# A convolution by DFTs and two gated MLPs on one core: inputs 4 to 15 of the transform come in quarters of 128 KB, not in halves of 256 KB

## The chip, the cores and the metric

One core of one Trainium2 chip. The metric is the device time of one execution in microseconds (us). The kernel before took 1119.01 us, the median of three runs (1118.45 to 1119.3).

## The reference

```
X = rfft(x, axis=1);  F = filt_r + 1j * filt_i            # x: 2 x 3008 x 256
y = irfft(X * F, n=3008, axis=1)                          # the transform: 16 inputs of 512 KB here
h = (silu(y @ w_gate) * (y @ w_val)) @ w_out              # 256 -> 1536 -> 256
g = h @ w_in
out = (g * clip(g + 3, 0, 6) / 6) @ w_out2                # 256 -> 2048 -> 256
```

All in float32 on 6016 tokens of 256 channels.

## The kernel before, in words

The sequence of 3008 is treated as a grid of 47 x 64. A transform **step** k (0 to 15) handles one batch and 32 channels: `over_n1` (DFT over the 47 rows, 64 small matmuls, L334), `over_n2` (over the 64 columns, 16 matmuls, L356), `filter_product` (VectorE and GpSimd multiply by the filter, L369), `back` (inverse over the columns, 16 matmuls, L383, ScalarE copies into `turned`, L388). The loop starts with `over_n1(k)`, then `back(k - 2)`, then the transfers that the table `moves` holds for step k, then `over_n2(k)` and `filter_product(k)`. After step 15 the results, which went through DRAM (tiles `d2_0`, `d2_1`, shown as `d`), are read back as `g`, `y` and `turned` tiles, `to_time` (L158) finishes the inverse, and the MLPs begin on TensorE (L234, L242, later L706 and L751), which are most of the time.

Everything is written in program order; no scheduler moves instructions. The transfers nearly all stand on SyncE's queue (SP), which issues them strictly in order; each waits until what it overwrites has been read. Every DMA also signals one of eight completion semaphores (DMAHW0 to DMAHW7 in the instruction order), handed out in turn, and waits at its issue until the transfer that used the same one, eight transfers earlier, has landed. So at most eight are on their way.

What the change and the prediction touch:

- `load_x(k)` (L286 to L295) brings input k, 512 KB, into the tile `ring`, which holds four inputs; input k + 3 is asked for in step k, after `over_n1(k)`, and overwrites input k - 1. Inputs 0 and 1 come with both halves of the channels in each piece, the others by channel halves.
- `load_filter(j)` (L299, 2 x 192 KB): filter 2 is asked for in step 2, filters 3 to 7 in steps 4 to 8. `prepare_filter` (L326, VectorE) uses it one or two steps later.
- `load_dec` (L406, 3 x 256 KB): the raw first weights, pieces in steps 1, 2, 3, then 8, 9, 9, then 12, 12, 13. ScalarE starts the first decoding in step 4 (L189).
- `store` (L392, 192 KB): parts of `turned` to DRAM, eight of the first channel half of batch 0 in steps 9 to 12, eight of the second in step 13.
- `load_half` (L464): reads them back; the second half's reads wait for all stores and are needed by `form(0, 1)` (L158 on `g`) right after `back(15)`.

Of the kernel before, what the change touches and what calls it, by code (L numbers as in the profile page):

```python
# [77 lines left out]
def fft_conv_glu_mlp(ctx: ExitStack, tc: tile.TileContext, x, filt, mats, sgn, w1, w2, out):  # L78
# [189 lines left out]
    with tc.manual_schedule():  # L268
# [17 lines left out]
        def load_x(k, engines=(nc.sync, nc.sync)):  # L286
            b, j = STEPS[k]
            if k % 2 == 0:
                xin[k // 2] = ring[:, k // 2 % RING * 2048:(k // 2 % RING + 1) * 2048].rearrange("p (a n) -> p a n", a=2)
            to, src = (v.rearrange("p (o i n) -> p i o n", o=2, i=2) if k < 2 else v.rearrange("p (i n) -> p i n", i=2)  # L290
                       for v in (xin[k // 2][:, k % 2], x[b, j // 2, :, j % 2]))
            for i in range(2):
                if (k, i) == (1, 1):
                    nc.sync.dma_start(out=mat[:, CO:], in_=mats[:, CO:])
                engines[i].dma_start(out=to[:, i], in_=src[:, i])  # L295

        def load_filter(j):
            for r in range(2):
                nc.sync.dma_start(out=fl[j // 4][:, j % 4, r], in_=filt[j][:, r])  # L299

        load_x(0, (nc.scalar, nc.sync))
        load_x(1, (nc.scalar, nc.sync))
        nc.sync.dma_start(out=sg, in_=sgn)
        load_filter(0)
        load_x(2)
        warm = keep.tile([P, 32], F32, name="warm")[:, 0:1]
        nc.gpsimd.memset(warm, 0.0)
# [282 lines left out]
        for t in range(2 * plain):  # L590
            p, i = divmod(t, 2)
            k, g_ = steps[p]
# [163 lines left out]
        class Plain:  # L756
            kind, k, f, n, last = 0, 0, 0, 512, True
# [105 lines left out]
        pieces = [(g, i) for g in range(G2) for i in range(2)]  # L863
# [19 lines left out]
        for s in range(S):  # L883
# [15 lines left out]
            k, f, n, kind = u.k, u.f, u.n, u.kind  # L899
# [73 lines left out]
        for j, accs in enumerate((banks["a"][1], banks["a"][3])):  # L973
            to, at = ys[k][:, ORDER.index(2 * j + 1), :n], pos[k] + n
# [52 lines left out]
```

## Time and profile before

| | |
|---|---|
| median of three runs | 1119.01 us |
| the profiled execution | 1118.54 us |
| its span (first to last instruction) | 1116.7 us |
| outside the span | 1.84 us |
| TensorE (PE) busy | 1107.7 us, 99% of the span |
| VectorE, ScalarE, GpSimd busy | 863.3, 750.4, 598.0 us |
| granted clock of TensorE | 0.999 |

The transform fills about the first 70 us. A row of the timeline gives start, length, engine, line, operation, tiles and count, and in brackets how long the engine stood idle before it and what ended that ("issue": nothing that the profile shows). PEld are TensorE's weight loads, SPq is SyncE's queue of DMA issues.

### The profile page before, as it was taken

The numbers are of one execution on the slowest core, as the hardware profiler recorded it, in microseconds if no ns is written. First come the engines' busy times: TensorE is split into PE (matmuls) and PEld (weight loads), VectorE is DVE, ScalarE is ACT, GpSimd is POOL, SyncE is SP. The second block draws the span as 40 slices with busy tenths as digits, with TensorE's granted clock in tenths as the row PEclk, the third lists the DMA queues.
The fourth block names the chain that finished last, engine by engine and source line by source line (L and its number), as shares of the span: only waits on it lengthen the run. The fifth ranks groups of instructions, "written<-read, shape, count | busy, mean of one in ns | idle before, by whom it ended". The sixth has DMA issues, their size and how long they took to land.

```text
span 1116.7 us, 19188 instructions
## 1 busy us (share of the span) xinstructions
PE 1107.7 (99%) x7237; PEld 921.4 (83%) x7237; DVE 863.3 (77%) x1179; ACT 750.4 (67%) x1363; POOL 598.0 (54%) x773
## 2 busy tenths in 40 slices
PE   8999999999999999999999999999999999999998
PEld 6778888888888888888899888888888888888997
DVE  5999977878878888786898868677677677677765
ACT  4655447667667667766777777777776677677764
POOL 3742376795865576474587645335435444354440
PEclk9999999999999999999999999999999999999999
DMA  8977845843733553273353421422322412412300
GB/s 272 286 222 227 256 157 170 232 143 131 192 121 113 155 165 100 83 203 113 103 207 111 171 81 55 152 78 77 129 78 78 145 61 78 149 52 78 116 27 33
DMA packets 58988, 150.75 MB, mean 135 GB/s; under 512 B 5712, under 2 KB 26160, under 8 KB 57136
## 3 DMA queue, kind: packets, MB, share of 16 engines
q1 hardware_dynamic: 58208, 148.78, 41.9%
q8 instruction: 56, 0.92, 0.4%
q10 hardware_dynamic: 688, 0.75, 0.2%
q14 instruction: 36, 0.29, 0.1%
HBM read 117.27 MB, written 32.24 MB: 134 GB/s over the span
## 4 chain that ended last, share of the span: by engine, by line
PE 93%; DVE 3%; DMA 2%; issue 1%; SPq 1%; ACT 0%; DVEq 0%; ACTq 0%
PE gv L706 44%; PE a L751 36%; PE gv L234 5%; PE a L242 3%; PE gv L158 1%; PE gv L383 1%; PE a L356 1%; PE gv L334 1%; DMA d<-turned 1%; DVE h L733 1%; DVE hs L116 1%; DMA ring<-x_in 0%; SPq L392 0%; DVE xs L116 0%; DMA g<-d 0%
## 5 line engine op out<-in xcount | busy, mean ns | idle before, releaser
L706 PE MATMUL gv<-xs,wu 128*128 128x512 f32 (+1 forms) x2268 | 567.1, 386 | 0.2 <-DVE gv L119 0.2
L116 POOL TENSOR_TENSOR wu<-st,wu 128x224 fp32r<-128x224 f32 x432 | 310.3, 749 | 396.2 <-ACT wu L539 396.2
L706 PEld LDWEIGHTS gv<-xs,wu 128*128 128x128 f32 x2268 | 423.6, 188 | 81.7 <-DVE h L119 1.8
L751 PE MATMUL a<-hs,wo 128*128 128x512 f32 (+1 forms) x1872 | 476.9, 385 | 0.0
L751 PEld LDWEIGHTS a<-hs,wo 128*128 128x128 f32 x1872 | 351.3, 188 | 65.6 <-ACT hs L739 0.3
L116 DVE TENSOR_TENSOR hs<-h,hs 128x512 fp32r<-128x512 f32 (+3 forms) x228 | 235.4, 1033 | 65.3 <-ACT hs L739 61.1
L739 ACT CAST hs<-h 128x512 fp32r<-128x512 f32 (+3 forms) x216 | 172.6, 799 | 130.0 <-DVE h L735 73.8
L116 POOL TENSOR_TENSOR wo<-st,wo 128x256 fp32r<-128x256 f32 x156 | 150.6, 978 | 0.0
L735 DVE SCALAR_TENSOR_TENSOR h<-h,gv 128x512 f32<-128x512 f32 (+1 forms) x144 | 96.5, 670 | 23.0 <-ACT h L729 22.8
L539 ACT CAST wu<-st 128x384 fp32r<-128x384 f32 x216 | 110.6, 563 | 0.6 <-DMA st<-w1f 0.6
L727 ACT ACTIVATE h<-gv 128x512 f32<-128x512 f32 (+1 forms) x120 | 70.6, 588 | 56.8 <-PE gv L706 55.6
L119 DVE TENSOR_TENSOR gv<-gv,h 128x512 f32<-128x512 f32 (+1 forms) x108 | 74.0, 685 | 40.2 <-PE gv L706 34.1
L729 ACT ACTIVATE h<-gv 128x512 f32<-128x512 f32 (+1 forms) x144 | 84.1, 584 | 15.5 <-PE gv L706 15.4
L916 ACT COPY gv<-gv 128x512 f32<-128x512 f32 (+1 forms) x108 | 60.9, 564 | 42.3 <-PE gv L706 38.5
L119 DVE TENSOR_TENSOR h<-gv,h 128x512 f32<-128x512 f32 (+1 forms) x108 | 73.0, 676 | 18.5 <-PE gv L706 17.9
L735 DVE SCALAR_TENSOR_TENSOR h<-h,h 128x512 f32<-128x512 f32 (+1 forms) x48 | 32.7, 681 | 58.6 <-ACT h L729 58.6
L920 ACT COPY h<-gv 128x512 f32<-128x512 f32 (+1 forms) x108 | 62.5, 579 | 15.8 <-PE gv L706 12.6
L733 DVE TENSOR_TENSOR h<-h 128x512 f32<-128x512 f32 (+1 forms) x60 | 61.5, 1024 | 1.7 <-ACT h L727 1.2
L116 DVE TENSOR_TENSOR xs<-raw,xs 128x512 fp32r<-128x512 f32 (+1 forms) x77 | 57.9, 753 | 0.1
L539 ACT CAST wo<-st 128x256 fp32r<-128x256 f32 (+1 forms) x108 | 54.1, 501 | 0.0
L582 ACT CAST xs<-raw 128x512 fp32r<-128x512 f32 (+1 forms) x77 | 45.7, 609 | 3.1 <-DVE raw L116 3.0
L234 PE MATMUL gv<-xs,wall_a 128*128 128x512 f32 x192 | 45.9, 393 | 0.2 <-ACT xs L123 0.2
(98 smaller groups left out, 893.9 us busy)
## 6 DMA issues: line engine op xcount, KB each, us to landing
st<-w1f SPq DMA_DIRECT2D x60, 576.0 KB, 3.8
st<-w2f SPq DMA_DIRECT2D x48, 704.0 KB, 4.1
raw<-w_in SPq DMA_DIRECT2D x16, 512.0 KB, 4.6
ring<-x_in SPq DMA_DIRECT2D x30, 256.0 KB, 5.2
x<-w_in SPq DMA_DIRECT2D x9, 768.0 KB, 5.6
yd<-y SPq DMA_DIRECT2D x5, 1024.0 KB, 6.7
raw<-yd SPq DMA_DIRECT2D x5, 1024.0 KB, 6.7
y_out<-y SPq DMA_DIRECT2D x20, 256.0 KB, 2.1
```

Source lines behind the costliest of these rows:

```text
L116: (engine or nc.vector).tensor_tensor(out=out, in0=a, in1=b, op=ALU.subtract)
L119: (engine or nc.vector).tensor_tensor(out=out, in0=a, in1=b, op=ALU.add)
L234: nc.tensor.matmul(acc, w[:, r, c[k]:c[k] + P], xs[:, v, k], start=(r, v, k) == (0, 0, 0), stop=(r, k) == (1, 1), skip_group_check=len(dep ...
L539: nc.scalar.copy(out=to[:, 0, at:at + hi - lo], in_=src[:, lo:hi])
L706: nc.tensor.matmul(acc[:, :n], w[:, r, FORM[a] * P:(FORM[a] + 1) * P], xs_part(k, v, i), start=start and q == 0, stop=q == 2, skip_group_c ...
L727: nc.scalar.activation(out=self.value(t, 0), in_=src, func=AF.Silu)
L729: nc.scalar.activation(out=self.value(t, a), in_=src, func=AF.Relu, bias=3.0)
L733: nc.vector.tensor_tensor(out=self.value(t, 0), in0=self.value(t, 0), in1=src, op=ALU.mult)
L735: nc.vector.scalar_tensor_tensor(out=self.value(t, a), in0=self.value(t, a), scalar=6.0, in1=src, op0=ALU.min, op1=ALU.mult)
L739: nc.scalar.copy(out=self.hs[:, t, :, 0, :self.n], in_=self.value(t))
L751: yield lambda t=t, v=v, a=a, j=j, r=r: nc.tensor.matmul(banks["a"][2 * j + t][:, :n], self.wo[:, r, (2 * a + j) * P:(2 * a + j + 1) * P], ...
L920: nc.scalar.copy(out=u.s7, in_=b3[:, :n])
```

## The change

For inputs 4 to 15 `load_x` cuts the 1024 floats of each partition into four pieces, not two, and issues the four DMAs one behind the other on SP. Inputs 0 to 3 stay as they are, and so does what each input brings and where it is put.

```diff
             b, j = STEPS[k]
             if k % 2 == 0:
                 xin[k // 2] = ring[:, k // 2 % RING * 2048:(k // 2 % RING + 1) * 2048].rearrange("p (a n) -> p a n", a=2)
-            to, src = (v.rearrange("p (o i n) -> p i o n", o=2, i=2) if k < 2 else v.rearrange("p (i n) -> p i n", i=2)
+            pieces = 2 if k < 4 else 4
+            to, src = (v.rearrange("p (o i n) -> p i o n", o=2, i=2) if k < 2 else v.rearrange("p (i n) -> p i n", i=pieces)
                        for v in (xin[k // 2][:, k % 2], x[b, j // 2, :, j % 2]))
-            for i in range(2):
+            for i in range(pieces):
                 if (k, i) == (1, 1):
                     nc.sync.dma_start(out=mat[:, CO:], in_=mats[:, CO:])
-                engines[i].dma_start(out=to[:, i], in_=src[:, i])
+                engines[i % 2].dma_start(out=to[:, i], in_=src[:, i])
```

SP's queue from input 4 on, in steps 1 and 2, before (128x512 on `ring` is half an input, `w_in` a piece of the raw first weights, `filt_in` half of a filter; in brackets the semaphores waited for, DMAHWn being the landing of the transfer eight places earlier):

```order
L295 DMA ring<-x_in 128x512 [waits DMAHW7_49,PE_49]
L295 DMA ring<-x_in 128x512 [waits DMAHW0_49,PE_49]
L406 DMA x_121<-w_in 128x512 [waits DMAHW1_49]
L295 DMA ring<-x_in 128x512 [waits DMAHW2_49,PE_49]
L295 DMA ring<-x_in 128x512 [waits DMAHW3_49,PE_49]
L406 DMA x_121<-w_in 128x512 [waits DMAHW4_49]
L299 DMA x_121<-filt_in 128x384 [waits DMAHW5_49]
L299 DMA x_121<-filt_in 128x384 [waits DMAHW6_49]
```

The same place in the changed kernel:

```order
L296 DMA ring<-x_in 128x256 [waits DMAHW7_49,PE_49]
L296 DMA ring<-x_in 128x256 [waits DMAHW0_49,PE_49]
L296 DMA ring<-x_in 128x256 [waits DMAHW1_49]
L296 DMA ring<-x_in 128x256 [waits DMAHW2_49,PE_49]
L407 DMA x_121<-w_in 128x512 [waits DMAHW3_49]
L296 DMA ring<-x_in 128x256 [waits DMAHW4_49,PE_49]
L296 DMA ring<-x_in 128x256 [waits DMAHW5_49,PE_49]
L296 DMA ring<-x_in 128x256 [waits DMAHW6_49]
L296 DMA ring<-x_in 128x256 [waits DMAHW7_49,PE_49]
L407 DMA x_121<-w_in 128x512 [waits DMAHW0_49]
L300 DMA x_121<-filt_in 128x384 [waits DMAHW1_49]
L300 DMA x_121<-filt_in 128x384 [waits DMAHW2_49]
```

Filter 2 moves back by four places on SP, and the transfer eight places ahead of it is now a quarter of input 4, not a half of input 3.

SP's queue at the end of the inputs, step 12, before (input 15, two pieces of weights, the last store of the first channel half, `d` from `turned`, and after the last weight piece the first read back):

```order
L295 DMA ring<-x_in 128x512 [waits DMAHW6_49,PE_49]
L295 DMA ring<-x_in 128x512 [waits DMAHW7_49,PE_49]
L406 DMA x_121<-w_in 128x512 [waits DMAHW0_49,DVE_49]
L406 DMA x_121<-w_in 128x512 [waits DMAHW1_49]
L392 DMA d_0_78<-turned 128x3x128 [waits DMAHW2_49]
L406 DMA x_121<-w_in 128x512 [waits DMAHW3_49]
L464 DMA g<-d_0_78 48x6x128 [waits DMAHW5_49,DMAHW4_49,DMAHW2_49]
```

And in the changed kernel:

```order
L296 DMA ring<-x_in 128x256 [waits DMAHW4_49,PE_49]
L296 DMA ring<-x_in 128x256 [waits DMAHW5_49,PE_49]
L296 DMA ring<-x_in 128x256 [waits DMAHW6_49]
L296 DMA ring<-x_in 128x256 [waits DMAHW7_49,PE_49]
L407 DMA x_121<-w_in 128x512 [waits DMAHW0_49,DVE_49]
L407 DMA x_121<-w_in 128x512 [waits DMAHW1_49]
L393 DMA d_0_78<-turned 128x3x128 [waits DMAHW2_49]
L407 DMA x_121<-w_in 128x512 [waits DMAHW3_49]
L465 DMA g<-d_0_78 48x6x128 [waits DMAHW4_49,DMAHW2_49]
```

By then 24 more DMAs have been issued (363 rows on SP, 339 before); the four of an input stand where two stood, and everything behind them keeps its order. The instructions of the other engines stay in their order.

## Rows read from the trace of the kernel before

**Rows 1.** The page, busy time, share of the span and instructions.

```profile
PE 1107.7 (99%) x7237; PEld 921.4 (83%) x7237; DVE 863.3 (77%) x1179; ACT 750.4 (67%) x1363; POOL 598.0 (54%) x773
```

**Rows 2.** Waits of TensorE, 8 to 75 us: us in total, times, longest.

```profile
PE a L356 <- issue: 2.2, 1, 2.2
PE gv L334 <- issue: 0.8, 1, 0.8
```

**Rows 3.** Timeline of TensorE, 17.3 to 20.5 us.

```profile
17.27 0.81 PE L356 MATMUL a<-y,mat 64*64 64x384 f32 x4
20.33 0.55 PE L356 MATMUL a<-y,mat 64*64 64x384 f32 x4 [2.25 <-issue]
```

**Rows 4.** Timeline of TensorE, 43 to 46 us.

```profile
45.33 0.39 PE L334 MATMUL gv<-mat,ring 48*64 48x48 f32 x12 [0.83 <-issue]
```

**Rows 5.** The page, DMA queues: packets, MB, share of 16 engines.

```profile
q8 instruction: 56, 0.92, 0.4%
```

**Rows 6.** DMA queues, 12 to 18 us.

```profile
q1 hardware_dynamic: 986, 1.76, 91.7%
```

**Rows 7.** DMA queues, 18 to 19.1 us.

```profile
q8 instruction: 1, 0.02, 5.5%
```

**Rows 8.** DMA queues, 43 to 44.1 us.

```profile
q8 instruction: 1, 0.02, 5.6%
```

**Rows 9.** Timeline of SP's issues, 8.2 to 13.5 us.

```profile
8.34 2.82 SPq L295 DMA_DIRECT2D ring<-x_in  x4
11.21 0.43 SPq L406 DMA_DIRECT2D x<-w_in  x1
11.73 0.86 SPq L295 DMA_DIRECT2D ring<-x_in  x2
```

**Rows 10.** Windows: engines' busy time (count), clock, DMA share, GB/s.

```profile
14.00:20.50 6.50, 4.25 (x106) 3.19 (x102) 3.37 (x8) 2.97 (x8) 2.83 (x6) 1.00 1.04 361
```

**Rows 11.** DMA packets by size, 6 to 7.5 us.

```profile
DMA packets 614, 0.56 MB, mean 371 GB/s; under 512 B 175, under 2 KB 611, under 8 KB 614
```

**Rows 12.** Waits of SP's queue, 8 to 55 us.

```profile
SPq L295 <- PE gv L334: 7.1, 8, 1.4
SPq L295 <- DMA ring<-x_in: 4.1, 4, 1.8
...
SPq L392 <- DMA ring<-x_in: 1.0, 3, 0.4
```

**Rows 13.** DMA issues, 16.5 to 17 us: KB each, median us to landing.

```profile
x<-w_in SPq DMA_DIRECT2D x1, 256.0 KB, 7.4
```

**Rows 14.** Timeline of ScalarE, 23.5 to 28 us.

```profile
24.79 0.95 ACT L189 ACTIVATE x<-x 128x768 f32<-128x768 f32 x1
26.45 0.48 ACT L347 COPY y<-gv 128x384 f32<-128x384 f32 x1 [0.72 <-PE gv L334]
26.83 0.34 ACT L348 ACTIVATE y<-gv 128x192 f32<-128x192 f32 x1
```

**Rows 15.** Chain of waits, 49 to 60 us: start, us, what.

```profile
51.26 6.02 DMA d<-turned
```

**Rows 16.** DMA issues, 68 to 69.7 us.

```profile
g<-d SPq DMA_DIRECT2D x2, 144.0 KB, 3.2
turned<-d SPq DMA_DIRECT2D x2, 144.0 KB, 4.3
```

**Rows 17.** Timeline, 58 to 80 us, SP's second reads and TensorE's use.

```profile
68.30 0.82 SPq L464 DMA_DIRECT2D g<-d  x2
...
73.64 0.84 PE L158 MATMUL a<-mat,g 48*64 48x47 f32 x48
```

**Rows 18.** Timeline of TensorE, two successive steps.

```profile
27.35 1.75 PE L356 MATMUL a<-y,mat 64*64 64x384 f32 x16
...
31.00 1.75 PE L356 MATMUL a<-y,mat 64*64 64x384 f32 x16
```

**Rows 19.** DMA issues, 0 to 60 us.

```profile
ring<-x_in SPq DMA_DIRECT2D x30, 256.0 KB, 5.2
```

## The prediction

> **What bounds the kernel now.** I read the busy times first: TensorE is busy for 99% of the span, no other engine over 77% [rows 1]. So time is won or lost only where TensorE stands still. The change touches the transform, and there the waits of TensorE say what there is to win: from 8 to 75 us it stood still for 2.2 us once and 0.8 us once, both put down to "issue", that is, to nothing that the profile shows; no wait for an input is among them [rows 2]. The inputs themselves come in time, so cutting them finer can't win by bringing the first quarter sooner.
>
> The two stalls need a reason. They are 2.25 us before 20.33 [rows 3] and 0.83 us before 45.33 [rows 4]. The DMA queue of kind "instruction", q8, moved 56 packets of together 0.92 MB [rows 5]; divided by the 7237 + 7237 instructions of TensorE and its weight loads that is 64 bytes each, and about 258 instructions a packet. So I take q8 for TensorE's own program. From 12 to 18 us no packet of it moved while q1, the data, had the DMA engines for 91.7% [rows 6]; one packet moved in the 1.1 us behind [rows 7], and TensorE went on at 20.33. The same stands before the second stall: one packet between 43 and 44.1 us [rows 8], TensorE going on at 45.33. My reading is that both stalls are a wait for the next piece of program, which came late behind queued data. That is inference from the times alone; the profile names no cause.
>
> How much data is queued? SP issued seven transfers of 256 KB from 8.34 to 12.59: four and two of `ring` and one of weights [rows 9]. From 14 to 20.5 us the DMA engines were full and moved 361 GB/s [rows 10].
>
> **The change, part by part.** Removed are 24 issues of 256 KB, added 48 of 128 KB: the bytes are the same, SP has 24 issues more.
>
> Moving the bytes. Rows of 1 KB per partition are half as long. Between 6 and 7.5 us nearly all packets were under 2 KB (611 of 614) and 371 GB/s were reached [rows 11], no less than the 361 with rows mostly of 2 KB. Bounds: no cost, or, if the extra completion of each transfer costs the engines a tenth of a microsecond (my estimate; no row isolates it), 0.2 us for each input. I take 0.1, beside other work unless the transfers are the bound.
>
> SP's time. Two issues of `ring` take 0.86 us [rows 9], so 0.43 each and 24 x 0.43 = 10.3 us more. What hides it is SP's own waiting between 8 and 55 us: 7.1 us for TensorE to free an input, and 4.1 and 1.0 us for a landing eight transfers back [rows 12], 12.2 us in these three rows. Sum: 10.3 against 12.2, so SP should end about as early, but with hardly any slack; in steps with seven issues it will run late by itself. Queued behind are filter 2, the weights, the stores and the read backs.
>
> The first stall. At the time when the missing program should have been asked for, about 12 us, seven transfers had gone out: 7 x 256 = 1792 KB. With the same rhythm of issues the changed kernel has sent two halves of input 3, four quarters of input 4 and one piece of weights: 2 x 256 + 4 x 128 + 256 = 1280 KB. 512 KB less, at 361 GB/s, is 1.45 us. So the stall should fall from 2.25 to 0.8 us if the program waits behind the data already queued. Bounds: 0, if it doesn't, and 2.25.
>
> The second stall. Again up to eight transfers are on their way and they are smaller, but which ones I can't read. Bounds 0 and 0.83; I take 0.5.
>
> What is late next. Two covers become thin. First, ScalarE's decoding of the first weights (24.79) needs the third weight piece, which was issued in the window at 16.5 us and took 7.4 us [rows 13], so it landed at about 24.0. The change puts 6 more issues ahead of it (two for each of inputs 4 to 6) but the same bytes; with 0.1 us for each input I take 24.3. Then ScalarE needs 0.95 for it and 0.48 + 0.34 for the next two copies, so it is at 26.07, where it was at 26.83 + 0.34 = 27.17 [rows 14]. TensorE can't come out of this place more than 1.1 us earlier than before, whatever it won at 18 us (0.7 to 1.4 for a landing 0.3 us to either side). Second, the read back of the second channel half: its reads start to go at 68.30, the last of them landing for `form(0, 1)` at about 68.67 + 3.5 = 72.1 (between the medians 3.2 and 4.3 [rows 16]), and TensorE uses them at 73.64 [rows 17]: 1.5 us of slack. That chain hangs on SP: the store at 51.26 that took 6.02 us [rows 15], then reads, eight stores, their landing. If SP issues that store S later, the slack is 1.5 - S. By the sum above S is small; I take 0.5, from -1 (shorter queue, quicker landing) to +3.
>
> Sum: 1.45 cut to 1.1 at the first place, plus 0.5, is 1.6; cut to 1.5 - 0.5 = 1.0 at the second. Everything behind is TensorE at work [rows 1], so 1.0 us should reach the end: the profiled execution's 1118.54 (span 1116.7 and 1.84 around it) goes to 1117.5. That execution is 0.47 us below the median of the three runs, so I forecast 1118.0.
>
> **The rivals.** (a) SP becomes the bound; this is the slower side. Successive steps of TensorE start 3.65 us apart [rows 18]. With eight transfers under way and seven to issue in each of steps 8 to 12 (four quarters and three others), SP keeps up only if a transfer lands within 8 x 3.65 / 7 = 4.2 us. The 256 KB halves took 5.2 us [rows 19]; 144 KB took 3.2 to 4.3 us [rows 16]. If the quarters still took 5.2 us, because the queue is full all the time, a step of seven would last 7 x 5.2 / 8 = 4.55 us, 0.9 late, and a step of six (4 to 7) 3.9, 0.25 late: 5 x 0.9 + 4 x 0.25 = 5.5 us late at the store, 5.5 - 1.5 = 4.0 us of TensorE waiting before 73.64: 1123.0. Against it: fewer bytes are queued, so landings should be quicker. It decides in favour of slower from S = 1.5 + 2.2 = 3.7 on.
>
> (b) The program's wait is not a matter of how much is queued. Then the stalls stay and the finer cut only uses up slack: 1119.0, up to half a microsecond either way. For it: from 12 to 18 us data moved all the time, and still not one packet of q8 among 986 [rows 6], so its lateness may have a reason of its own. The Trainium skill ("DMA: Bandwidth & Descriptors", section on queues, rings and completion order) says that each DMA engine takes turns between the queue rows it has work for, packet by packet; by that a fetch would wait for a packet or so and never behind seven transfers, and this case would be the likely one. The trace doesn't look like it if the fetch was asked for before 18 us; when it was asked for no row shows.
>
> (c) Both stalls go, and neither cover gets in the way, because smaller transfers also land sooner: 2.25 + 0.83 = 3.1 us, 1115.9. For it: the bounds allow it. Against it: both thin covers would have to gain over 1.5 us at the same time.
>
> **How the numbers follow.** Forecast 0.48, (a) 0.15, (b) 0.24, (c) 0.13. A measurement of this kernel can tell about 0.2%, 2.2 us, from no change: faster than 1116.8 means (c) and the edge of the forecast, 0.15; slower than 1121.2 means (a), 0.15 with its weak forms left out and the forecast's own edge put in; the rest, 0.70, lies within. The range: below, the forecast with the full first cut and no second (2.25 less than the median) and part of (c), 1116.2; above, (b) with S = 3 (1.5 us more) and the start of (a), 1121.0. That leaves about 0.1 on either side.
>
> **What would show it.** Right: the wait before `over_n2(3)` at about 18 us is under 1.5 us and a packet of q8 lies before 18 us; SP's waits for TensorE nearly gone; ScalarE waiting for a weight piece before L189; the last store of the first half issued within a microsecond of 51.3; the landing of the quarters well under 5.2 us. Wrong: the stall still 2 us or more (then the queue's length is not its cause), a new idle time of TensorE before `form(0, 1)` of several microseconds (then SP is the bound), TensorE waiting for `ring`, or a new stall put down to "issue" elsewhere, which would be program fetches late at other places; the sum has no term for that last one.

## The result and the profile after

The changed kernel took 1125.01 us (median of six runs, 1123.71 to 1125.94); the kernel before, run beside it on the same chip, 1118.92 us. The ratio is 1.0053 (95% interval 1.004 to 1.0066): 0.5% slower. The time forecast, 1118.0, and its range up to 1121.0 were both missed.

The profiled execution took 1125.94 us with a span of 1124.2; before it was 1116.7, so 7.5 us are to be found. TensorE is still the busiest engine, and is even busy for longer than in [rows 1] (the page, busy time):

```profile
PE 1111.1 (99%) x7237; PEld 922.6 (82%) x7237; DVE 862.5 (77%) x1179; ACT 750.4 (67%) x1363; POOL 597.2 (53%) x773
```

The same number of instructions, 3.4 us more busy time: some of them ran slower. Where they did is shown below. First the waits of TensorE from 8 to 85 us (us in total, times, longest), to be held against [rows 2]:

```profile
PE gv L234 <- DVE xs L116: 5.2, 1, 5.2
PE a L357 <- ACT y L348: 2.1, 2, 1.3
PE gv L384 <- DVE h L116: 0.3, 1, 0.3
```

Both stalls of the kernel before are gone, 3.1 us together. In their place TensorE waits for ScalarE twice (1.26 and 0.83 us) and for VectorE once (5.22 us), 7.3 us together; all its waits in these 77 us are 7.6 us, against 3.5 before.

**The two waits for ScalarE** are the cover of the weights. ScalarE's timeline, 23 to 29 us, against [rows 14]:

```profile
24.92 0.90 ACT L189 ACTIVATE x<-x 128x768 f32<-128x768 f32 x1 [2.72 <-DMA x<-w_in]
25.72 0.47 ACT L348 COPY y<-gv 128x384 f32<-128x384 f32 x1
```

The third piece of the first weights came at 24.9 us, ScalarE had stood idle for 2.72 us, the copy that TensorE needs was queued behind it, and TensorE waited 1.26 us, until 26.24. The same happened with the second weights (L189 at 49.01, TensorE 0.83 us before 50.33).

**The wait for VectorE** is the large one. VectorE's timeline, 68 to 78 us:

```profile
69.13 0.89 DVE L198 TENSOR_SCALAR x<-x 128x768 f32<-128x768 f32 x1
75.49 0.56 DVE L200 TENSOR_SCALAR x<-x 128x768 uint32<-128x768 uint32 x1 [5.47 <-DMA w1f<-x]
75.97 1.41 DVE L116 TENSOR_TENSOR xs<-a,xs 128x256 fp32r<-128x256 f32 x4
```

L198 and L200 are two steps of the decoding of the second weights. L200 writes the tile from which the decoded first weights are stored to DRAM (`w1f`, L413, the transfer that `KEEP = 14` puts behind the eight stores of step 13), so it has to wait until that store has read it. Behind L200 in VectorE's order stands the subtraction L116 whose result `xs` is what TensorE multiplies at L234. In the kernel before L200 ran at 70.09, and the store had landed at 69.08: a slack of 1.0 us that nobody sees, because nothing waits.

**Why that store is late** stands in SP's issues, 48 to 76 us (start, length until the last of them was issued, count):

```profile
54.48 3.62 SPq L296 DMA_DIRECT2D ring<-x_in  x4
58.19 0.87 SPq L407 DMA_DIRECT2D x<-w_in  x2
59.11 0.43 SPq L393 DMA_DIRECT2D d<-turned  x1
59.58 0.48 SPq L407 DMA_DIRECT2D x<-w_in  x1
63.01 1.34 SPq L465 DMA_DIRECT2D g<-d  x2
64.39 0.96 SPq L465 DMA_DIRECT2D y<-d  x2
65.45 5.48 SPq L393 DMA_DIRECT2D d<-turned  x8
71.02 0.47 SPq L413 DMA_DIRECT2D w1f<-x  x1
```

The last store of the first channel half was issued at 59.11; before it was 51.26 [rows 15]: 7.85 us late. The read back has to wait for its landing, and the eight stores and the store of `w1f` come behind: `w1f` was issued at 71.02 and landed 4.38 us later, at 75.40, 6.3 us behind the kernel before (64.77 and 69.08). Less 1.0 us of slack that is the 5.3 us that L200, and with it TensorE, waited.

**The slower instructions** are those behind that wait. Windows of all engines (stretch, its length, then busy time and count of TensorE, its weight loads, VectorE, ScalarE and GpSimd; the third number from the end is TensorE's granted clock, behind it DMA share and GB/s):

```profile
71.60:76.80 5.20, 0.03 (x1) 0.03 (x1) 1.31 (x4) 0.00 (x0) 0.00 (x0) 0.90 0.62 191
76.80:82.00 5.20, 5.20 (x67) 2.93 (x67) 2.87 (x5) 0.86 (x2) 0.00 (x0) 0.50 0.94 285
82.40:82.80 0.40, 0.40 (x3) 0.26 (x3) 0.37 (x2) 0.27 (x1) 0.00 (x0) 0.77 0.00 0
82.80:83.20 0.40, 0.40 (x3) 0.35 (x2) 0.40 (x3) 0.00 (x0) 0.00 (x0) 1.00 0.00 0
```

TensorE came out of the wait at a granted clock of 0.50, that is 1.2 and not 2.4 GHz, and had 1.00 again from about 82.6 us on. The read back's 48 matmuls, 0.84 us in [rows 17], took 1.43:

```profile
80.54 1.43 PE L158 MATMUL a<-mat,g 48*64 48x47 f32 x48
```

TensorE worked at half clock from 76.77 to 82.59, and 5.8 us at half clock are 2.9 us of work lost. In the kernel before the clock is 1.00 over the same stretch.

The account: waits of 7.6 us against 3.5 are 4.1 us more, and the clock took 2.9; that is 7.0 of the 7.5 us. The rest is spread too thin for these views.

### The profile page after: what moved, and what is told of

Read it like the earlier page. It is cut to its first block, busy times and chain, and to the rows that moved or that the text cites. A ratio compares the mean times of both kernels' runs of the same rounds, so it can differ in the third digit from the quotient of the medians.

```text
span 1124.2 us, 19222 instructions
## 1 busy us (share of the span) xinstructions
PE 1111.1 (99%) x7237; PEld 922.6 (82%) x7237; DVE 862.5 (77%) x1179; ACT 750.4 (67%) x1363; POOL 597.2 (53%) x773
## 4 chain that ended last, share of the span: by engine, by line
PE 94%; DVE 2%; DMA 2%; issue 1%; SPq 1%; ACT 0%; DVEq 0%; ACTq 0%
PE gv L707 44%; PE a L752 36%; PE gv L234 6%; PE a L242 3%; PE gv L384 2%; PE gv L158 1%; PE a L357 1%; PE gv L335 1%; DMA x<-w_in 1%; DVE h L734 1%; DVE hs L116 0%; DMA ring<-x_in 0%; SPq L393 0%; DMA w1f<-x 0%; DVE xs L116 0%
## 5 line engine op out<-in xcount | busy, mean ns | idle before, releaser
L116 POOL TENSOR_TENSOR wu<-st,wu 128x224 fp32r<-128x224 f32 x432 | 311.7, 753 | 396.7 <-ACT wu L540 396.7
L116 DVE TENSOR_TENSOR hs<-h,hs 128x512 fp32r<-128x512 f32 (+3 forms) x228 | 235.8, 1034 | 65.7 <-ACT hs L740 62.0
L116 POOL TENSOR_TENSOR wo<-st,wo 128x256 fp32r<-128x256 f32 x156 | 150.8, 979 | 0.0
L116 DVE TENSOR_TENSOR xs<-raw,xs 128x512 fp32r<-128x512 f32 (+1 forms) x77 | 58.0, 754 | 0.1
L234 PE MATMUL gv<-xs,wall_a 128*128 128x512 f32 x192 | 46.7, 397 | 5.2 <-DVE xs L116 5.2
```

What stands on the lines that cost most here:

```text
L116: (engine or nc.vector).tensor_tensor(out=out, in0=a, in1=b, op=ALU.subtract)
L234: nc.tensor.matmul(acc, w[:, r, c[k]:c[k] + P], xs[:, v, k], start=(r, v, k) == (0, 0, 0), stop=(r, k) == (1, 1), skip_group_check=len(dep ...
```

## Where SP's time went

The prediction held 10.3 us of added issues against 12.2 us of SP's waits. I added up SP's single issues in both traces, from the same one (the last piece of filter 1, issued at 7.87 and at 7.37) to the last store of the first half; an issue of over 0.65 us counts with 0.45 as ordinary, and the rest of it as "lengthened".

| SP, to the last store of the first half | before | after |
|---|---|---|
| issues | 55 | 79 |
| their ordinary time | 21.8 us | 32.6 us |
| lengthened | 5.9 us | 11.2 us |
| gaps between issues | 16.1 us | 8.4 us |
| in all | 43.8 us | 52.2 us |

The added issues cost 10.7 us, nearly as forecast. But only 7.7 us of the gaps were used for them, and 5.3 us came on top in issues that took 0.7 to 2.9 us in place of 0.43. What these have in common is the program's queue. SP's issues from 8 to 20 us:

```profile
11.82 0.42 SPq L407 DMA_DIRECT2D x<-w_in  x1
12.33 4.31 SPq L296 DMA_DIRECT2D ring<-x_in  x4
16.70 0.42 SPq L407 DMA_DIRECT2D x<-w_in  x1
17.17 0.90 SPq L300 DMA_DIRECT2D x<-filt_in  x2
```

The four quarters at 12.33 should take 1.7 us; three of them did, and one stood from 13.76 to 16.64. The DMA queues between 13 and 16.7 us:

```profile
q1 hardware_dynamic: 827, 0.87, 73.0%
q8 instruction: 1, 0.02, 4.2%
```

4.2% of 16 engines over 3.7 us are 2.5 us for this one packet of q8, which stood from 13.77 to 16.28. The same holds at 23.96 to 26.00 (packet 24.07 to 25.63), 50.03 to 51.77 (49.71 to 51.35) and 56.24 to 58.10 (56.21 to 57.73); in all 10 of the 11 long issues overlap a packet of q8, and 7 of 8 in the kernel before. In the changed kernel each of the ten packets of this stretch overlaps a long issue; before, one of eight (18.07 to 19.03) fell mostly into a gap, and the issue at its start took no longer than 0.33 us. That the two coincide is shown. What holds the issue up is not: no experiment took a packet of q8 away.

## The experiments

Two accounts stood against each other. Mine after the result: the loss is the number of issues on SP, which is out of slack in steps 8 to 12, and the end of the chain is L200's wait for the store of `w1f`. The rivals: shorter rows make the transfers dearer; or the bytes come in a worse order for the stalls. All ratios are to the kernel before on the same chip.

### e1_rows1k: the changed kernel's short rows, the number of issues as before

```diff
-to, src = (v.rearrange("p (o i n) -> p i o n", o=2, i=2) if k < 2 else v.rearrange("p (i n) -> p i n", i=2)
+to, src = (v.rearrange("p (o i n) -> p i o n", o=2, i=2) if k < 2 or k >= 4 else v.rearrange("p (i n) -> p i n", i=2)
```

> Two transfers of 256 KB for each input as before, but each takes a quarter of both channel halves, so its rows are 1 KB as in the changed kernel. If the number of SP's issues makes the loss: as before, 1118.9 within 0.7 us, with the stall at 18 us still about 2.2 us and the last store of the first half issued at 51 to 52 us. If the short rows make it (slower transfers): 1122 to 1125, and landings of ring over 5.5 us.

1118.23 us, ratio 0.9995 [0.9985, 1.0004]; the last store was issued at 50.79 us. Rows of 1 KB cost nothing that these runs can tell. The first stall was 1.0 us, not the 2.2 expected. That is not much outside what e4 and e9 below show: their inputs 4 to 6 come as in the kernel before, and they stood 1.4 us there.

### e2_parts: the number of issues as after, rows of 2 KB

```diff
-                engines[i].dma_start(out=to[:, i], in_=src[:, i])
+                for q in ((slice(0, P),) if k < 4 else (slice(0, 64), slice(64, P))):
+                    engines[i].dma_start(out=to[q, i], in_=src[q, i])
```

> Four transfers of 128 KB for inputs 4 to 15 as in the changed kernel, but each takes 64 partitions with rows of 2 KB. If the number of issues makes the loss: 1124 to 1126, the last store of the first half at 58 to 60 us and TensorE waiting about 5 us for VectorE's xs near 76 us. If the short rows make it: near 1119.

1129.22 us, ratio 1.0101 [1.0085, 1.0116]: nearly twice the loss, with the long rows, and more than either account had expected. SP's issues at 26 us of this kernel, and of the changed kernel:

```profile
26.93 2.39 SPq L296 DMA_DIRECT2D ring<-x_in  x4
```

```profile
26.10 1.80 SPq L296 DMA_DIRECT2D ring<-x_in  x4
```

That is 0.60 us from one issue to the next on 64 partitions and 0.45 on 128; the single issue of `ring` took 0.55 and 0.38 us (medians). The last store was issued at 62.79, 3.7 us later still, although these transfers landed in 4.0 us, sooner than the 4.5 of the changed kernel. The time at the issue decides, not the time to the landing.

### e8_tiny: the halves of before, and a transfer of 4 KB behind each of the 24

```diff
                 engines[i].dma_start(out=to[:, i], in_=src[:, i])
+                if k >= 4:
+                    nc.sync.dma_start(out=spare[:, (2 * k + i - 8) * 8:(2 * k + i - 8) * 8 + 8], in_=x[0, 0, :, 0, :8])
```

> The kernel before with halves, and behind each half of inputs 4 to 15 a transfer of 4 KB into a tile that nothing reads: 24 more issues, no more data worth counting. If the issues and the eight places make the loss: 1122 to 1126, the last store of the first half at 56 us or later. If the cutting of the data makes it: 1118.5 to 1119.5.

1126.7 us, ratio 1.0077 [1.0062, 1.0092]. The data comes as in the kernel before, and 96 KB more in a tile that nobody reads; 24 issues alone bring the whole loss and more (7.7 us between the medians, just over the range expected), and by the same way. Waits of TensorE, 8 to 85 us, and of VectorE, 60 to 82 us:

```profile
PE gv L234 <- DVE xs L116: 5.7, 1, 5.7
PE a L359 <- ACT y L350: 2.4, 2, 1.4
```

```profile
DVE x L200 <- DMA w1f<-x: 6.5, 1, 6.5
```

The first stall was gone here too: spreading the halves in time does what cutting them does.

### e6_fewer and e7_fewer_halves: 14 issues less, with the quarters and with the halves

Both bring filters 2 to 7 in one transfer of 384 KB each and store batch 0 in 8 transfers of 384 KB, not 16 of 192; e6 has the quarters of the change, e7 the halves.

```diff
         def load_filter(j):
+            if j >= 2:
+                nc.sync.dma_start(out=fl[j // 4][:, j % 4], in_=filt[j])
+                return
...
-        for i in range(8):
-            send((9, 10, 10, 10, 11, 11, 11, 12)[i], store, 0, 0, i)
-            send(13, store, 0, 1, i)
+        for i in range(4):
+            send((9, 10, 11, 12)[i], store, 0, 0, i, 4)
+            send(13, store, 0, 1, i, 4)
```

> The changed kernel with quarters kept, but filters 2 to 7 in one transfer of 384 KB each, not two, and the sixteen stores of batch 0 in eight of 384 KB: 14 issues fewer on SP (10 of them ahead of the w1f store's place in step 12, 4 among the step 13 stores). If SP's issues make the loss: the last store of the first half goes out about 5 us earlier than in the changed kernel, the waits near 76 us shrink from 5.2 to under 1 us, 1118 to 1120. If it is the quarters themselves: 1124 to 1126.

> The kernel before (halves) with the same merging of filters and stores. SP has slack there, so merging alone should give little: 1118 to 1119.5; the two stalls of 2.25 and 0.83 us, which hang on the data queued ahead of TensorE's program, stay or grow by up to 1 us because the merged transfers are larger.

e6: 1119.09 us, 1.0007 [0.9995, 1.0019], where the change alone gave 1.0053: taking issues away elsewhere wins back the loss, with the quarters as they are. Its last store was issued at 53.05 us. All waits of TensorE, 8 to 85 us:

```profile
PE gv L338 <- issue: 1.0, 1, 1.0
PE gv L387 <- DVE h L116: 0.3, 1, 0.3
PE gv L234 <- ACT xs L123: 0.2, 1, 0.2
```

The profiled execution of e6 has a span of 1115.6 us, 1.1 less than before, but it was the fastest of ten runs that spread from 1117.41 to 1122.44, and their median shows no gain. e7: 1118.94 us, 0.9999 [0.999, 1.0009], and both stalls stay (2.5 and 0.6 us), so fewer issues alone neither help the kernel before nor touch its stalls.

### e3_first2, e4_mid and e9_late: quarters for some of the inputs

On the changed kernel; the three lines with a plus are e3, e4 and e9, in this order.

```diff
-            pieces = 2 if k < 4 else 4
+            pieces = 4 if k in (4, 5) else 2
+            pieces = 4 if 7 <= k < 11 else 2
+            pieces = 4 if k >= 11 else 2
```

> Quarters for inputs 4 and 5 alone, halves for the rest: 4 more issues than before. If the first stall hangs on how much data is queued when TensorE's program is fetched, and the loss on SP's 24 issues: the stall of 2.25 us before 20 us is gone or under 0.5, the store at 51.3 us is late by under 1 us, and the time is 1117.2 to 1118.2. If the stall hangs on something else: 1118.9 to 1119.5.

> Quarters for inputs 7 to 10 alone, which are asked for in the steps that have six issues on SP. If SP falls behind only where a step has seven issues: the last store of the first half within 1.5 us of 51.3 us, the stall at 18 us still there, 1118.5 to 1119.5. If every finer input costs the same (6.1 us for twelve): four cost 2 us, 1121.

> Quarters for inputs 11 to 15 alone, asked for in steps 8 to 12, where SP then has seven issues a step: 10 more issues than before. If SP falls behind where a step has seven issues (four quarters for inputs 7 to 10, with six, cost nothing): the last store of the first half 1.5 to 4 us later than 51.3 us, TensorE waiting 0.5 to 3 us near 72 us, 1119.5 to 1122. If it needs all 24 issues, the early ones too: 1118.5 to 1119.3.

| | added issues | last store issued | `w1f` waited for | us | ratio |
|---|---|---|---|---|---|
| e3, inputs 4, 5 | 4 | 52.60 | no | 1117.76 | 0.9991 [0.9981, 1.0001] |
| e4, inputs 7 to 10 | 8 | 52.74 | 0.8 us | 1118.65 | 0.9995 [0.9985, 1.0005] |
| e9, inputs 11 to 15 | 10 | 56.25 | 2.1 us | 1123.23 | 1.0033 [1.0019, 1.0047] |

The added issues of e3 stand in steps 1 and 2; its store was 1.3 us late, where under 1 was expected. Eight more in steps 4 to 7, where SP has gaps, lose nothing, though VectorE's wait of 0.8 us for the store of `w1f` says that the slack is just used up; ten in steps 8 to 12, where it has seven things to issue per step, lose 4.6 us between the medians (3.7 by the ratio; the runs spread from 1119.01 to 1125.84), more than I had expected at most. TensorE waited 1.8 us for VectorE in e9, but the clock was lost again, as this window of e9, and behind it that of the kernel before, show (70 to 85 us):

```profile
70.00:85.00 15.00, 12.88 (x241) 8.73 (x233) 9.68 (x18) 6.64 (x16) 3.32 (x5) 0.89 0.67 202
```

```profile
70.00:85.00 15.00, 14.77 (x173) 10.69 (x166) 12.93 (x23) 7.01 (x16) 3.23 (x3) 1.00 0.73 215
```

0.11 of 15 us are 1.7 us, nearly as much as the wait itself. In e3 the first stall was gone, as its cause asks: only the inputs queued before 18 us matter for it.

### e5_keep12: the changed kernel with the store of `w1f` ahead of the read back

```diff
-        KEEP = 14
+        KEEP = 12
```

> The changed kernel with the store of the first decoded weights (w1f, L413) sent in step 12, ahead of the read backs and the eight stores of step 13, not behind them. If VectorE's wait of 5.5 us for that store is what holds TensorE at 76 us: that wait is gone, and TensorE next waits for the read back of the second half (landing near 78.6 us) before form(0, 1): about 2 us better than the changed kernel, 1122.5 to 1123.5. If the read back was the real bound all along: 1124.5 to 1125.5.

1123.69 us, ratio 1.0043 [1.0029, 1.0057]. The time is 1.3 us under the changed kernel's, which the two intervals don't separate (1.0053 [1.004, 1.0066]); what the trace shows is the order of the waits. L200 no longer waits (68.40), and the next wait stands right behind. TensorE, 68 to 84 us:

```profile
73.28 1.52 PE L384 MATMUL gv<-h,mat 64*64 64x384 f32 x16
77.56 0.31 PE L158 MATMUL a<-mat,g 48*64 48x47 f32 x2 [2.76 <-DMA g<-d]
78.38 0.89 PE L158 MATMUL a<-mat,g 48*64 48x47 f32 x46 [0.50 <-DMA g<-d]
```

That is `form(0, 1)` waiting for the read back, the place that the prediction had named. Here the granted clock fell to 0.50 twice, from 69.64 and from 79.88 for 3.4 us each, so the clock took more (3.4 us) than in the changed kernel (2.9), though TensorE waited less.

### e12_first2_again, e10_first2_fewer and e11_first2_dec5: is there a gain to be had?

e12 is e3 once more, with more rounds. e10 is e3 with the fewer issues of e6. e11 is e3 with ScalarE's first decoding (L189) a step later:

```diff
-        for f, steps in ((0, (4, 5, 6, 6, 7, 8, 9, 10, 10)), (1, (10, 11, 11, 12, 12, 13, 14, 15, 17)), (2, (15, 15, 15, 17))):
+        for f, steps in ((0, (5, 5, 6, 6, 7, 8, 9, 10, 10)), (1, (10, 11, 11, 12, 12, 13, 14, 15, 17)), (2, (15, 15, 15, 17))):
```

> Quarters for inputs 4 and 5 alone, once more with more rounds, since its interval (0.9981 to 1.0001) just touched 1. If the lost first stall is a true gain: ratio 0.9985 to 0.9995 with an interval below 1. If not: 0.9995 to 1.0005.

> Quarters for inputs 4 and 5 alone, with filters 2 to 7 and the stores of batch 0 merged: 4 issues more and 10 fewer ahead of the end of step 12. If the first stall goes with less data queued and SP keeps its slack: the stall at 18 us under 0.7 us, no wait near 72 us, 1116.8 to 1118. If the merged filters queue as much data as the quarters saved: 1118.5 to 1119.3.

> Quarters for inputs 4 and 5 alone, and ScalarE starts the decoding of the first weights (L189) in step 5, not 4. With the quarters alone TensorE waited 1.6 us for ScalarE, which I put down to the third weight piece landing too late for step 4. If so: that wait is gone, L189 waits for no DMA, and the time is 0.5 to 1.3 us under that of the quarters alone, 1116.5 to 1117.3 beside 1118.8 for the kernel before. If the gain is taken back elsewhere (program fetches, the read back): as the quarters alone, 1117.5 to 1118.3.

e12: 1117.95 us, 0.9993 [0.9984, 1.0002]; with e3 that is twice 0.6 to 1.1 us faster and twice an interval that reaches 1. e10: 1120.37 us, 1.0012 [1.0003, 1.0021], a miss and if anything slower: the stall before 20 us was gone, but TensorE waited 2.5 us for "issue" at two other places. e11: 1118.49 us, 0.9993 [0.9984, 1.0002], outside both ranges expected: ScalarE's wait for the weights was gone, and a new stall stood behind it. (The execution traced here took 1120.92 us, the slowest of eleven; the fastest took 1116.22.) TensorE of e11, 28 to 33 us:

```profile
30.94 0.46 PE L335 MATMUL gv<-mat,ring 48*64 48x48 f32 x11 [2.99 <-issue]
```

And the DMA queues of e11 from 27.9 to 31 us, again one packet of q8 among full data traffic:

```profile
q1 hardware_dynamic: 598, 0.96, 92.3%
q8 instruction: 1, 0.02, 2.2%
```

So the first stall can be taken away at the price of four issues, but in the executions traced what is won there is given back at the weights (e3, e12) or at the next late packet of program (e10, e11). There is one trace for each kernel, and those of e3, e11 and e12 are of executions slower than their median, so how often it is given back isn't shown. No version measured here is clearly faster than the kernel before.

## Why the prediction was wrong

**What bounds the kernel, and the two stalls: right.** Both went, and the first for the reason given. The DMA queues of the changed kernel from 12 to 18 us, where [rows 6] had no packet of q8 at all:

```profile
q1 hardware_dynamic: 1224, 1.28, 69.7%
q8 instruction: 1, 0.02, 2.6%
```

The traces show more than the prediction could infer. The kernel before up to each of its two stalls, with TensorE's matmuls and weight loads counted in brackets (first two numbers):

```profile
0.00:20.20 20.20, 16.42 (x348) 10.91 (x349) 9.90 (x24) 7.20 (x18) 4.82 (x13) 1.00 0.88 277
0.00:45.20 45.20, 40.59 (x985) 29.93 (x986) 30.56 (x60) 20.76 (x55) 21.95 (x37) 1.00 0.89 276
```

In the 14 traces TensorE stood for "issue" over 0.3 us 22 times, and only ever at the same seven places of its program: after 445, 697, 952, 1207, 1716, 1971 or 2735 matmuls and weight loads, about 255 apart or two or three times that. Each time it went on 1.3 to 1.6 us after the end of a packet of q8. So q8 does carry TensorE's program, and these stalls are waits for its next piece.

For the first stall the traces also tell what the piece waited for. By 13.75 to 14.4 us all 14 kernels had started 511 matmuls and weight loads; in the changed kernel the packet began at that moment, 13.77, so it was asked for no later. Where 1351 to 1669 KB of data had then been issued and not yet moved (before, e1, e4, e7, e9), it began 2.6 to 4.3 us after that moment and TensorE stood 1.0 to 2.5 us for it; where it was 627 to 954 KB (the others), 0.0 to 2.1 us after, and TensorE stood 0.3 us at most. That holds for the long rows of e2 and e8 and for the short rows of e1, so it is the bytes queued and not the length of the rows. At the later packets the relation is looser, and why one is late there stays open. The cut was taken too small, 1.45 of 2.25 us: the changed kernel had 971 KB less waiting (660 against 1631), not the 512 KB counted.

**Moving the bytes: right.** e1 puts the cost of the short rows at nothing (0.9995). The quarters landed in 4.5 us, against 5.2 [rows 19]. The 0.1 us taken for each input's extra completions is shown by no run.

**The cover of the weights: right** as a place, and as a size by luck. ScalarE ended up there waiting for the third piece, until 24.92 where 24.3 was forecast, and TensorE came out of it at 26.24, where it was at 27.35 [rows 18]: the 1.1 us earlier that I had set as the most. A landing 0.6 us later should have left 0.5 of it by my own sum; but that sum counted two copies, and TensorE went on after the first, which ended at 26.19. The second weights were a second such cover that I hadn't looked for.

**SP's time: this step failed.** "SP should end about as early" was taken as S = 0.5, with a range to 3; S was 7.85 at the last store, though the same paragraph says that steps with seven issues would run late by themselves. Two things were wrong in it. I set the sum of added issues against the sum of SP's waits over the whole stretch, as though a gap in step 3 could pay for an issue in step 12; e4 and e9 show that it can't. And SP's own lengthened issues were no term at all, though the trace of before had 5.9 us of them: the four issues at 8.34 took 2.82 us [rows 9], where four of 0.43 take 1.7, in plain sight.

**What is late next: the wrong place.** The slack that I counted was that of the read back, 1.5 us [rows 17]. The store of `w1f` had 1.0 us, and it is queued behind the same eight stores. It hangs on a tile that is written again, so nothing in the waits of before points to it; I would have found it by asking of each transfer behind the late one, who overwrites what it reads. e5 shows both places, the second right behind the first.

**The clock: a term that was missing.** TensorE's wait cost 2.9 us more than its length.

**The rivals.** (a), SP as the bound, is what happened, at 1125.0 for its 1123.0; but its mechanism was another, and so near a time is luck. It had SP held up by landings, and asked for one within 4.2 us. The quarters took 4.5, yet SP's waits for landings were 1.2 us in all from 36 to 60 us (of its waits in that window, the three for a DMA):

```profile
SPq L296 <- DMA ring<-x_in: 0.8, 1, 0.8
SPq L393 <- DMA x<-w_in: 0.2, 1, 0.2
SPq L407 <- DMA x<-w_in: 0.2, 1, 0.2
```

From 49.52 to the last store its issues stand one behind the other without a gap of over 0.1 us, and e2, with landings of 4.0 us, was later still. What bound SP was the time of the issues themselves. (a) also lacked the clock (2.9 us) and the nearer cover. I gave it 0.15 because fewer queued bytes should land sooner. They did, by 0.7 us, and that did not matter. (b) fell: the stalls went, and how late the packet came followed the bytes queued. The sentence from the Trainium skill ("DMA: Bandwidth & Descriptors", queues, rings and completion order) that spoke for (b) is not borne out here: by turns, packet by packet, a fetch would not be late by microseconds, and in the kernel before it began 4.1 us after the instruction at which the changed kernel's did, with 1.4 MB of data moved in between. (c) asked both covers to gain over 1.5 us; one gained nothing beyond 1.1 and the other went the wrong way.

The Trainium skill ("DMA: Bandwidth & Descriptors", section "Issuing engines are not separate DMA queues") says that the time a sequencer takes to start a DMA is usually small relative to the DMA. Against one landing it is (0.43 of 4.5 us). Summed over a queue that has seven of them to issue in a step of 3.65 us [rows 18], it was the bound: 7 x 0.43 is 3.0 us before a single one is lengthened.

## What to carry to other kernels

Before a transfer is cut, add up the issues of its queue step by step, not over the whole stretch: gaps in one step don't pay for another, and a queue at 80% of its step has no slack, since single issues can take much longer than their median (up to 2.9 us for 0.43 here). Then follow the late queue down to every transfer behind, and ask for each one both who reads what it brings and who overwrites what it takes; the second kind of slack shows in no list of waits. And price a wait of TensorE with what the clock takes behind it.

## What the runs showed of the hardware

- A DMA issue on SP mostly took 0.33 to 0.45 us for 128 partitions and about 0.55 for 64 (e2), for 256 KB as for the 4 KB of e8 (median 0.43). Of the 11 issues of 0.7 to 2.9 us in the changed kernel, 10 overlapped a packet of the program's queue.
- The granted clock was 0.50 behind waits of 5.2 us (after), 2.5 us (e7) and 1.8 us (e9), for 5.8 us of TensorE's work in the first case and 3.4 in the others. Behind the stall of 2.25 us in the kernel before [rows 3] it stayed at 1.00. So the length of a wait alone doesn't tell what it costs.
- A packet of q8 is 0.92 MB / 56 = 16 KB [rows 5], and TensorE's stalls for it lie about 255 matmuls and weight loads apart. The Trainium skill ("Runtime: NRT & Kernel Launch", section "Instruction fetch mechanics") says that each engine fetches its program in blocks of 16 KiB, 256 instructions, ahead of use and hidden behind the issue of the current ones. The size agrees; hidden it was not here, with stalls of 0.3 to 3.0 us behind late packets.
